# A gated linear recurrence and a top-1 expert layer on one core: transfers with their own planned rates, loads in quarters, heads moved in two long pieces

## The chip, the core and the metric

The kernel runs on one core of a Trainium2 chip. The core has TensorE (PE, with its weight loads shown apart as PEld), VectorE (DVE), ScalarE (ACT), GpSimd (POOL) and SyncE (SP); SP does nothing here but issue DMAs, in the order in which they stand in its queue. The metric is the device time of one execution in microseconds (us), lower being better. All data is float32.

## The reference, cut to what matters

The first half is a recurrence over 768 steps for 4 batches x 8 heads x 48 channels; its output, with heads side by side, is 3072 tokens of 384 values. The second half sends each token to the one expert (of 8) with the highest gate logit.

```python
mag = np.sqrt(a_re * a_re + a_im * a_im)
scale = np.minimum(mag, 0.999) / (mag + 1e-06)          # a = a * scale
for t in range(S):                                      # S = 768
    S_re, S_im = ar*S_re - ai*S_im + k v^T,  ar*S_im + ai*S_re
    y[:, :, t] = einsum('bhd,bhde->bhe', q[:, :, t], S_re)
x = y.transpose(0, 2, 1, 3).reshape(B * S, H * D)       # 3072 x 384
logits = x @ w_gate;  e = argmax(logits);  g = softmax(logits)[e]
out = g * (relu(x @ w1[e]) @ w2[e])                     # w1 384x1024, w2 1024x384
```

## The kernel before, in words

**Attention.** The recurrence is done in chunks of 128 steps: within a chunk by matrices, between chunks by a state. The sequence work is cut into ten units (`UNITS`): u0 (128 steps), u1 (256), six full units u2 to u7 of 384 steps, u8 (256) and u9 (128). For each unit `front(u)` loads a_re and a_im in one DMA into the tile `AB`, and q and k in one DMA into `Z` (`ld`, line 280); there are two buffers of each, shown as AB_124 and Z_126 for even units and AB_125 and Z_127 for odd ones. Then ACT, DVE and POOL turn the gates into magnitudes and angles: Ln and Exp on ACT, the product im*c on POOL, a square with its maximum on DVE (line 291), Ln, an add (295), Exp, a clamp (299), the running sum `D` (scan, line 301), two Exp, the products K on DVE and Q on POOL (the latter the last reader of `AB`), the arc tangent, the running angle `cs` (scan, line 312), sine and cosine. Four DVE products per unit write `zp` (line 326): part 1 (imaginary) from the sine, then part 0 from the cosine, each for k and q. `zp`, `D` and `cs` have one buffer each.

**Moves.** The channels stand on 128 partitions in blocks (`BLOCKS`), the matrix work wants each head on 96 rows. So ten DMAs per unit, five for each part, move `zp` to `hz` inside SBUF (line 333): four of 48 partitions, two of 32, four of 16. `hz` has two buffers (hz_147, hz_148). `chunk(b, c)` then does the matrix work of each of the 24 chunks on PE: transposes of k (line 363), scores (370), state reads (382), values (389), state update (397) and the turn to tokens with the logits (405). DVE masks the scores into `am`, ACT copies the rest. `route` finds each token's expert and place, and POOL scatters the rows to `xs_hbm` (line 467).

**Order.** Nothing of this is ordered by hand. `Plan` collects operations with an engine, a duration, a latency and, for transfers, kilobytes; `order()` makes a list schedule over all engines, in which transfers share one wire at 0.30 KB per ns (`RATE`), and the kernel emits the instructions in the order of the planned starts. `after=` adds a pure ordering: the loads of unit u are planned after the moves of unit u-2.

**Experts.** Between the two halves a check (lines 513 to 536) finds whether a general, slow path must be run (it is not run here); its tiles come from a pool `chkp`, in the memory that the attention's tiles leave, and the expert tiles then use the same memory. For each expert rows `xr` and weights `w1b`, `w2b` are loaded, rows are transposed (587), multiplied by w1 (598), by w2 (612), scaled and scattered to the output. This half is ordered by a second `Plan`.

Of the kernel before, what the change touches and what calls it, by code (L numbers as in the profile page):

```python
# [9 lines left out]
FP32 = mybir.dt.float32  # L10
# [12 lines left out]
G = 3  # L23
# [20 lines left out]
class Plan:  # L44
# [5 lines left out]
    def add(self, eng, dur, fn, r=(), w=(), tag=None, lat=0.0, kb=0.0, prio=0.0, port=False, after=()):  # L50
# [16 lines left out]
        self.ops.append(dict(i=i, eng=eng, dur=dur, fn=fn, deps=sorted(deps), tag=tag, lat=lat, kb=kb, bump=prio, port=port, after=after,  # L67
# [3 lines left out]
    XL, TBL, RATE, SLACK = 0.12, 1.3, 0.30, 0.05  # L71
# [13 lines left out]
    def tails(self, succ):  # L85
        tail = [0.0] * len(self.ops)
        for o in reversed(self.ops):
            t = max([us + tail[s] for s, us, data in succ[o["i"]] if data], default=0.0)
            tail[o["i"]] = t + o["dur"] + o["kb"] / self.RATE / 1e3 + o["bump"]
        return tail  # L90

    def run(self, prio, edges, ins, back, stick):
# [4 lines left out]
        cur, dma, per_kb = None, 0.0, 1 / self.RATE / 1e3  # L97
# [5 lines left out]
        for _ in ops:  # L103
# [27 lines left out]
            if o["kb"] and not back:  # L131
                dma = end = max(dma, end) + o["kb"] * per_kb
            for s, us, data in edges[i]:
                ready[s] = max(ready[s], end + us + (ops[s]["kb"] * per_kb if back else 0.0) if data else issued)
                n[s] -= 1
                if n[s] == 0:
                    cand[ops[s]["eng"]].append(s)
# [19 lines left out]
def gateloop_then_moe(ctx, tc, gates, qk, v, wg, w1, w2, out):  # L157
# [57 lines left out]
    with ExitStack() as att:  # L215
# [8 lines left out]
        zp, = buf("zp", 1, [128, 2, TU // 128, 2, G, 128])  # L224
# [6 lines left out]
        hz = buf("hz", 2, [96, TU // 128, 2, H, 128])  # L231
# [29 lines left out]

        def front(u):
# [16 lines left out]
            def ld(o, src, keys):  # L279
                P.add("SP", 0.65, lambda: nc.sync.dma_start(o[:, :, :, sl], src[b, :, :, :, t0:t1]), (), keys, lat=1.5, kb=2 * n * 0.512, after=moved[u - 2] if u > 1 else ())  # L280
# [43 lines left out]
            for part, key, tr in ((1, Sk, si), (0, ("co",), co)):  # L324
                for x, xk, src in ((1, K, kk), (0, Q, qq)):
                    P.add("DVE", dve2(n), lambda part=part, tr=tr, x=x, src=src: tt(
                        zp[:, part, 0:nch, x].rearrange("p c g t -> p g c t"), src.rearrange("p g (c t) -> p g c t", t=128),
                        tr.rearrange("p g (c t) -> p g c t", t=128), ALU.mult), (xk,) + tuple(key), (("zp", part, x),), port=True)
            for part in (1, 0):
                for p0, p1, g0, g1, h0, d0 in BLOCKS:  # L330
                    m, r0 = g1 - g0, part * D + d0
                    eng, dma = ("ACT", nc.scalar) if u == 0 and part == 0 and h0 else ("SP", nc.sync)
                    i = P.add(eng, 0.65, lambda dma=dma, p0=p0, p1=p1, g0=g0, g1=g1, h0=h0, r0=r0, m=m, part=part: dma.dma_start(
                        hz[slot][r0:r0 + p1 - p0, cl:cl + nch, :, h0:h0 + m].rearrange("p c x h t -> p (c x) h t"),
                        zp[p0:p1, part, 0:nch, :, g0:g1].rearrange("p c x g t -> p (c x) g t")),
                        (("zp", part, 0), ("zp", part, 1)), tuple(("h", slot, cl + x, h, part, d0) for x in range(nch) for h in range(h0, h0 + m)),
                        lat=1.6, kb=2 * (p1 - p0) * m * T * 4 / 1e3)
# [7 lines left out]
        def chunk(b, c):  # L345
# [7 lines left out]
            hq, hk = hz[slot][:, cl, 0], hz[slot][:, cl, 1]  # L353
# [60 lines left out]
        def route(b, r0, r1):  # L414
# [50 lines left out]
            for c in range(n):  # L465
# [6 lines left out]
                P.add("POOL", 1.27, f, (slot, ("xg", (g0 + c) % XR), ("empty", 0), ("empty", 1), ("empty", 2)), (("rows", b, r0 + c),), lat=2.0, kb=197)  # L472
# [14 lines left out]
        with tc.manual_schedule():  # L487
            for u in range(NU):
# [4 lines left out]
                if u == 3:  # L493
                    for h in range(3):
                        P.add("SP", 0.65, lambda h=h: nc.sync.dma_start(
                            xs_hbm.rearrange("(e s) w -> s e w", e=E)[MINC + 64 * h:MINC + 64 * h + 64],
                            bc(empty[0:64, None, :], [64, E, W])), (), (("empty", h),), lat=2, kb=E * 64 * W * 4 / 1e3, after=moved[1])
                for c in range(t0 // 128, t1 // 128):
                    chunk(b, c)
# [12 lines left out]
    with ExitStack() as fs:  # L512
        fp = fs.enter_context(tc.tile_pool(name="chkp", bufs=1, reuse_waits="tile"))
        ok = fp.tile([128, 4], FP32, name="ok")
        f1 = fp.tile([128, NU], FP32, name="f1")
        nc.vector.tensor_scalar(out=f1, in0=chk, scalar1=2.25, scalar2=None, op0=ALU.is_le)
        nc.vector.tensor_reduce(ok[:, 0:1], f1, axis=AX, op=ALU.min)
        lv = lend.rearrange("p b g c -> p (b g) c")
        f2 = fp.tile([128, B * G, C], FP32, name="f2")
        tt(f2, lv[:, :, 1:], lv[:, :, :C], ALU.subtract)  # L520
        nc.vector.tensor_scalar(out=f2, in0=f2, scalar1=-60.0, scalar2=None, op0=ALU.is_ge)
        nc.vector.tensor_reduce(ok[:, 1:2], f2.rearrange("p a c -> p (a c)"), axis=AX, op=ALU.min)
        f3 = fp.tile([128, B * G], FP32, name="f3")
        nc.vector.tensor_scalar(out=f3, in0=lv[:, :, C], scalar1=-100.0, scalar2=None, op0=ALU.is_ge)
        nc.vector.tensor_reduce(ok[:, 2:3], f3, axis=AX, op=ALU.min)
        nc.tensor.matmul(bank[7][:, 0:E], lhsT=ones_b, rhs=cumb, start=True, stop=True)
        f4 = fp.tile([128, E], FP32, name="f4")
        nc.vector.tensor_scalar(out=f4, in0=bank[7][:, 0:E], scalar1=float(CAP), scalar2=None, op0=ALU.is_le)
        f5 = fp.tile([128, E], FP32, name="f5")
# [264 lines left out]
```

## Time and profile before

| | us |
|---|---|
| median of 3 runs | 621.64 (617.7 to 622.54) |
| the profiled execution | 618.8 |
| its span, first to last instruction | 617.0 |
| span of the attention half, to its last matrix work | about 293 |
| pause of TensorE between the halves | 297.7 to 306.8 |
| expert half | 310 to 617 |

| engine | busy in the span | share |
|---|---|---|
| PE | 520.4 | 84% |
| DVE | 261.0 | 42% |
| ACT | 207.6 | 34% |
| POOL | 104.3 | 17% |

Busy shares mix two halves with different limits, so each half is read by itself. "Idle before" a row, and the releaser named with it, say what the engine waited for. The DMA share is the mean busy share of the core's 16 DMA engines; it counts a packet that waits for memory as busy. PEclk is the granted TensorE clock as a share of full speed: 0.50 is 1.2 GHz, 1.00 is 2.4 GHz.

### The profile page before, as it was taken

What the parts mean: (1) busy time and instruction counts of PE and PEld (TensorE: products, weight loads), DVE (VectorE), ACT (ScalarE), POOL (GpSimd) and SP (SyncE); (2) the same over time, 40 slices, a digit from 0 to 9 for tenths busy, and PEclk for the clock granted to TensorE, in tenths of its full rate; (3) what the DMA queues carried; (4) which work ended last, traced back from release to release, by engine and by line L of the source; (5) the groups of instructions that cost most, each with busy time, mean ns of one, the idle gap of its engine ahead of it and who ended that gap; (6) DMA issues with size and microseconds to landing.
All of it is one profiled execution on the core that took longest, in us unless ns stands there. A gap on an engine that the chain in (4) does not pass through costs nothing. (4 is left out here: it accounts for less than half of the span.)

```text
span 617.0 us, 7130 instructions
## 1 busy us (share of the span) xinstructions
PE 520.4 (84%) x2785; PEld 361.0 (59%) x2785; DVE 261.0 (42%) x460; ACT 207.6 (34%) x287; POOL 104.3 (17%) x112
## 2 busy tenths in 40 slices
PE   0269179976979695999199999999999999999996
PEld 0259169865868695988155555555555555555553
DVE  4957955995865954884212021111111111111111
ACT  6665755873847464774011000110001100011000
POOL 5113022303411214233200011100101011100011
PEclk9999655975957668799589999999999999999999
DMA  6584597758797948263795041630425301310000
GB/s 193 159 217 161 107 238 131 216 106 203 181 284 169 174 129 202 55 147 111 268 406 195 13 163 49 242 109 13 167 93 196 109 25 65 115 56 1 13 35 31
DMA packets 47080, 85.57 MB, mean 139 GB/s; under 512 B 3760, under 2 KB 42704, under 8 KB 44992
## 3 DMA queue, kind: packets, MB, share of 16 engines
q1 hardware_dynamic: 43424, 75.33, 44.2%
q0 software_dynamic: 3328, 9.47, 4.3%
q8 instruction: 24, 0.39, 0.3%
q10 hardware_dynamic: 288, 0.25, 0.2%
q14 instruction: 16, 0.13, 0.1%
HBM read 54.32 MB, written 12.62 MB: 109 GB/s over the span
## 5 line engine op out<-in xcount | busy, mean ns | idle before, releaser
L598 PE MATMUL bank<-xrt,w1b 128*128 128x448 f32 x384 | 148.4, 542 | 0.0
L612 PE MATMUL bank<-w2b,ht 128*128 128x384 f32 x384 | 127.5, 488 | 0.0
L598 PEld LDWEIGHTS bank<-xrt,w1b 128*128 128x128 f32 x384 | 73.3, 192 | 68.4 <-issue 64.7
L612 PEld LDWEIGHTS bank<-w2b,ht 128*128 128x128 f32 x384 | 72.5, 190 | 50.5 <-issue 4.1
L370 PE MATMUL bank<-hz 96*128 96x128 f32 x384 | 71.7, 352 | 32.9 <-DMA hz<-zp 31.6
L370 PEld LDWEIGHTS bank<-hz 96*128 96x128 f32 x384 | 64.2, 255 | 39.0 <-issue 24.0
L604 ACT ACTIVATE ht<-bank 128x448 f32<-128x448 f32 x32 | 17.4, 543 | 178.6 <-PE bank L598 178.6
L556 POOL DMA_INDIRECT out_dram<-yo,xr x24 | 23.5, 980 | 283.4 <-DVE yo L567 280.9
L601 DVE TENSOR_SCALAR ht<-bank 128x448 f32<-128x448 f32 x32 | 20.0, 624 | 111.1 <-PE bank L598 104.2
L363 PE MATMUL bank<-ident,hz 96*128 96x96 f32 x160 | 26.3, 314 | 38.3 <-DMA hz<-zp 38.3
L567 DVE TENSOR_SCALAR yo<-bank,xr 128x384 f32<-128x384 f32 x24 | 14.8, 618 | 103.2 <-PE bank L612 103.2
L363 PEld LDWEIGHTS bank<-ident,hz 96*128 96x128 f32 x160 | 21.5, 186 | 41.3 <-issue 31.9
L507 ACT ACT_TABLE_LOAD x35 | 44.9, 1283 | 1.4 <-PEq L782 0.8
L170 DVE TENSOR_TENSOR am<-bank,causal 128x512 f32<-128x512 f32 x48 | 32.2, 685 | 29.3 <-PE bank L370 29.2
L170 DVE TENSOR_TENSOR zp<-Z,cs 128x1152 f32<-128x1152 f32 (+2 forms) x40 | 42.6, 1111 | 0.7 <-ACT cs L254 0.6
L170 POOL TENSOR_TENSOR Z<-Z,AB 128x1152 f32<-128x1152 f32 (+2 forms) x9 | 22.5, 2504 | 102.3 <-ACT AB L254 51.6
L397 PEld LDWEIGHTS bank<-v,kt 128*96 128x96 f32 x320 | 36.8, 202 | 3.4 <-issue 2.8
L397 PE MATMUL bank<-v,kt 128*96 128x48 f32 x320 | 38.4, 284 | 0.4 <-ACT sb L401 0.4
L170 POOL TENSOR_TENSOR AB<-AB,C 128x1152 f32<-128x1152 f32 (+2 forms) x9 | 22.0, 2446 | 98.1 <-ACT C L254 86.6
L589 ACT COPY xrt<-bank 128x384 f32<-128x384 f32 x16 | 7.6, 478 | 86.4 <-PE bank L587 86.4
L405 PE MATMUL bank<-turn,yt 128*128 128x104 f32 x192 | 33.4, 330 | 3.3 <-ACT xg L409 1.8
L389 PE MATMUL bank<-am,v 128*48 128x128 f32 x384 | 33.9, 328 | 0.0
(112 smaller groups left out, 517.1 us busy)
## 6 DMA issues: line engine op xcount, KB each, us to landing
w1b<-in_w_dram SPq DMA_DIRECT2D x8, 1536.0 KB, 7.4
w2b<-in_w_dram SPq DMA_DIRECT2D x8, 1536.0 KB, 8.5
hz<-zp SPq DMA_DIRECT2D x24, 432.0 KB, 6.7
AB<-in_gates_dram SPq DMA_DIRECT2D x6, 1152.0 KB, 6.6
Z<-in_qk_dram SPq DMA_DIRECT2D x6, 1152.0 KB, 10.5
xr<-xs_hbm SPq DMA_DIRECT2D x8, 579.0 KB, 3.8
v<-in_v_dram SPq DMA_DIRECT2D x8, 576.0 KB, 10.2
xs_hbm<-empty SPq DMA_DIRECT2D x3, 772.0 KB, 13.2
```

The costliest lines, as they stand in the source:

```text
L170: (eng or nc.vector).tensor_tensor(out=o, in0=a, in1=b, op=op)
L363: nc.tensor.transpose(KT[hf][:, (h % 4) * 96:(h % 4) * 96 + 96], hk[:, h], ident[0:96, 0:96])
L370: nc.tensor.matmul(SC[hf][:, (h % 4) * 128:(h % 4) * 128 + 128], lhsT=hk[:, h], rhs=hq[:, h], start=True, stop=True)
L389: nc.tensor.matmul(YT[ps, (h // 2) * 128:(h // 2) * 128 + 128], lhsT=V[:, cl, h * D:h * D + D], rhs=am[2 * par + hf][:, h % 4, :], start=( ...
L397: nc.tensor.matmul(ST[0:96, h * D:h * D + D], lhsT=kt[par][:, h * 96:h * 96 + 96], rhs=V[:, cl, h * D:h * D + D], start=(c == 0 and h == 0 ...
L405: nc.tensor.matmul(XT[:, p * 104:p * 104 + 104], lhsT=yt[par][:, p * 128:p * 128 + 128], rhs=turn[:, p, :], start=True, stop=True)
L507: nc.scalar.preload_act_table_set("natural_log_exp_and_others" if P.cur == "LE" else "trig_and_small")
L556: i = nc.gpsimd.indirect_dma_start(out=out[:, :], out_offset=bass.IndirectOffsetOnAxis(ap=index, axis=0), in_=y, in_offset=None, bounds_ch ...
L598: nc.tensor.matmul(HB[hb][:, 0:CAP], lhsT=w1b[ws][:, c:c + 128], rhs=xrt[s][:, d, :], start=(d == 0), stop=(d == DT - 1))
L601: M.add("DVE", 0.6, lambda f_=f_, hb=hb: nc.vector.tensor_scalar_max(ht[s][:, f_, :], HB[hb][:, 0:CAP], 0.0), (("H", hb),), (("ht", s, f_),))
L604: M.add("ACT", 0.6, lambda f_=f_, hb=hb: nc.scalar.activation(ht[s][:, f_, :], HB[hb][:, 0:CAP], func=ACT.Relu), (("H", hb),), (("ht", s, ...
L612: nc.tensor.matmul(OB[ob][:, 0:DM], lhsT=ht[s][:, f_, j * 128:j * 128 + 128], rhs=w2b[ws][:, f_ * DM:f_ * DM + DM], start=(f_ == 0), stop= ...
```

## The change

Five things change. (1) The planner's `kb` and common rate become `wire`, a time of its own for each kind of transfer: loads at 0.32, moves at 0.213 KB per ns, values 1.9 us, weights 4.0 us instead of 5.2. (2) A load of a unit becomes two DMAs, one for each of a_re, a_im, q, k, and the inputs lie in HBM by half sequences, so that a partition's row of a full unit is one run of 4608 bytes and not three of 1536; the `after=` of the loads and of the values is gone. (3) `zp` and `hz` hold a full unit as (part of q or k, head, step), so that a move has two pieces of up to 4608 bytes per partition and not six of up to 1536; partial units keep the old layout. (4) The check's tiles come from `consts`, memory of their own. (5) The general path reads the new input layout.

```diff
-    XL, TBL, RATE, SLACK = 0.12, 1.3, 0.30, 0.05
+    XL, TBL, SLACK = 0.12, 1.3, 0.05
-            if o["kb"] and not back:
-                dma = end = max(dma, end) + o["kb"] * per_kb
+            if o["wire"] and not back:
+                dma = end = max(dma, end) + o["wire"]
...
+        def operand(t, full, z, c):
+            if full:
+                return t.rearrange("p (z h t) -> p z h t", z=2, h=H)[:, z, :, c * 128:c * 128 + 128]
+            return t.rearrange("p (c z h t) -> p c z h t", z=2, h=H, t=128)[:, c, z]
...
             def ld(o, src, keys):
-                P.add("SP", 0.65, lambda: nc.sync.dma_start(o[:, :, :, sl], src[b, :, :, :, t0:t1]), (), keys, lat=1.5, kb=2 * n * 0.512, after=moved[u - 2] if u > 1 else ())
+                for x in range(2):
+                    P.add("SP", 0.65, lambda x=x: nc.sync.dma_start(
+                        o[:, x, :, sl], src[b, t0 // TU, :, x, :, t0 % TU:t0 % TU + T]), (), keys[x:x + 1], lat=1.6, wire=n * 0.000512 / 0.32)
...
+                        if T == TU:
+                            o, i = o.rearrange("p (z x) -> p z x", z=2), i.rearrange("p (z x) -> p z x", z=2)
+                            dma.dma_start(o[:, :, h0 * T:(h0 + m) * T], i[:, :, g0 * T:g1 * T])
...
-                        lat=1.6, kb=2 * (p1 - p0) * m * T * 4 / 1e3)
+                        lat=1.6, wire=2 * (p1 - p0) * m * T * 4e-6 / 0.213)
...
-            P.add("SP", 0.08, lambda: nc.sync.dma_start(
-                vb[i % 3], v[b, 3 * half:3 * half + 3].rearrange("c p f -> p c f")), (), (("v", i % 3),), lat=1.9, kb=590, after=moved.get(2 * b + half - 1, ()))
+            P.add("SP", 0.65, lambda: nc.sync.dma_start(
+                vb[i % 3], v[b, 3 * half:3 * half + 3].rearrange("c p f -> p c f")), (), (("v", i % 3),), lat=1.6, wire=1.9)
...
-        fp = fs.enter_context(tc.tile_pool(name="chkp", bufs=1, reuse_waits="tile"))
-        ok = fp.tile([128, 4], FP32, name="ok")
+    ok = consts.tile([128, 4], FP32, name="ok")
...
-            M.add("SP", 0.65, lambda: nc.sync.dma_start(w1b[ws], w1[e * 128:e * 128 + 128, :]), (), (("w1", ws),), lat=1.9, kb=1573,
+            M.add("SP", 0.65, lambda: nc.sync.dma_start(w1b[ws], w1[e * 128:e * 128 + 128, :]), (), (("w1", ws),), lat=1.9, wire=4.0,
```

**SP's queue in the middle of the attention half.** Before, from the loads of u4 (AB_124, Z_126) to those of u5 (AB_125, Z_127), with the ten moves of u3 (into hz_147) between them; a load is a whole unit:

```order
L280 DMA AB_124<-in_gates_dram 128x6x384
L280 DMA Z_126<-in_qk_dram 128x6x384
L342 DMA v_133<-in_v_dram 128x3x384
L333 DMA hz_147<-zp_132 48x6x384 x2
L333 DMA hz_147<-zp_132 32x6x256
L333 DMA hz_147<-zp_132 16x6x128 x2
L333 DMA hz_147<-zp_132 48x6x384 x2
L333 DMA hz_147<-zp_132 32x6x256
L333 DMA hz_147<-zp_132 16x6x128 x2
L280 DMA AB_125<-in_gates_dram 128x6x384
L280 DMA Z_127<-in_qk_dram 128x6x384
```

Now, around the ten moves of u2 (into hz_148); AB_124 and Z_126 are loads of u4, AB_125 of u5, and each row is a half:

```order
L287 DMA AB_124<-in_gates_dram 128x1152
L350 DMA hz_148<-zp_132 48x2x1152 x2
L350 DMA hz_148<-zp_132 32x2x768
L350 DMA hz_148<-zp_132 16x2x384 x2
L287 DMA AB_125<-in_gates_dram 128x1152
L287 DMA Z_126<-in_qk_dram 128x1152
L350 DMA hz_148<-zp_132 48x2x1152 x2
L350 DMA hz_148<-zp_132 32x2x768
L350 DMA hz_148<-zp_132 16x2x384 x2
L287 DMA Z_126<-in_qk_dram 128x1152
L361 DMA v_133<-in_v_dram 128x3x384
L287 DMA AB_125<-in_gates_dram 128x1152
```

The gates of u4 stand ahead of the moves of u2 and no longer behind them, the first half of u5's gates stands between the two parts of u2's moves, where before it stood behind all of u3's.

**DVE between the products `zp` of u2 and those of u3.** Rows that write cs or D at 128x384 are the scans. Before, the last product of u2 (Z_126) and the twelve rows from it on; the products of u3 come four rows later:

```order
L170 TENSOR_TENSOR zp_132<-Z_126,cs_131 128x3x3x128
L312 SCALAR_TENSOR_TENSOR cs_131<-bank_68,tend,AB_125 128x384 x3
L299 TENSOR_SCALAR AB_125<-AB_125 128x1152
L301 SCALAR_TENSOR_TENSOR D_130<-AB_125,lend,C_129 128x384 x3
L283 COPY tend<-cs_131 128x3x3
L317 TENSOR_SCALAR cs_131<-cs_131 128x1152
L318 SCALAR_TENSOR_TENSOR cs_131<-cs_131 128x1152
L320 TENSOR_SCALAR cs_131<-cs_131 128x1152
L170 TENSOR_TENSOR Z_127<-Z_127,C_129 128x1152
L411 TENSOR_REDUCE lg<-bank_67 128x8
L170 TENSOR_TENSOR am_138<-bank_61,causal 128x512
L170 TENSOR_TENSOR am_139<-bank_62,causal 128x512
```

Now, from the last two products of u2 to those of u3:

```order
L170 TENSOR_TENSOR zp_132<-Z_126,cs_131 128x1152 x2
L303 SCALAR_TENSOR_TENSOR AB_124<-C_128,AB_124 128x1152
L170 TENSOR_TENSOR Z_127<-Z_127,C_129 128x1152
L325 TENSOR_SCALAR cs_131<-cs_131 128x1152
L326 SCALAR_TENSOR_TENSOR cs_131<-cs_131 128x1152
L430 TENSOR_REDUCE lg<-bank_67 128x8 x2
L328 TENSOR_SCALAR cs_131<-cs_131 128x1152
L307 TENSOR_SCALAR AB_124<-AB_124 128x1152
L309 SCALAR_TENSOR_TENSOR D_130<-AB_124,lend,C_128 128x384 x2
L170 TENSOR_TENSOR am_138<-bank_61,causal 128x512
L309 SCALAR_TENSOR_TENSOR D_130<-AB_124,lend,C_128 128x384
L170 TENSOR_TENSOR zp_132<-Z_127,cs_131 128x1152 x4
```

Both scans of u3 (from AB_125) have moved ahead of the last products of u2; in their place stand the add, the clamp and one scan of u4 (AB_124).

**SP's queue at the head of the expert half.** Before, the first row is w1's first load:

```order
L573 DMA w1b_2011<-in_w_dram 128x3072
L576 DMA xr_2017<-xs_hbm 128x3x386
L579 DMA xr_2017<-xs_hbm 64x386
L576 DMA xr_2018<-xs_hbm 128x3x386
L575 DMA w2b_2014<-in_w_dram 128x3072
```

Now the first expert's rows come first:

```order
L593 DMA xr_2039<-xs_hbm 128x3x386
L590 DMA w1b_2033<-in_w_dram 128x3072
L596 DMA xr_2039<-xs_hbm 64x386
L593 DMA xr_2040<-xs_hbm 128x3x386
L592 DMA w2b_2036<-in_w_dram 128x3072
```

The load of w1 has moved behind the rows that the last scatter writes.

## Rows read from the trace of the kernel before

**Rows 1.** Busy time in three stretches: start:end, length, PE, PEld, DVE, ACT, POOL, PEclk, DMA share, GB/s.
```profile
0.00:293.00 293.00, 214.96 (x1788) 194.69 (x1789) 211.51 (x348) 182.19 (x238) 73.72 (x80) 0.80 0.69 168
310.00:617.00 307.00, 301.69 (x980) 163.73 (x978) 44.80 (x82) 23.75 (x46) 27.43 (x28) 0.99 0.28 103
```
**Rows 2.** Who waited for whom, attention half: total us, times, longest.
```profile
POOL AB L170 <- ACT C L254: 86.6, 8, 21.1
...
PE bank L370 <- DMA hz<-zp: 31.6, 9, 14.9
...
SPq L333 <- DVE zp L170: 122.1, 11, 22.5
```
**Rows 3.** SP's queue in time: start, length, what, count.
```profile
94.51 14.33 SPq L333 DMA_DIRECT2D hz<-zp  x10
108.94 0.60 SPq L280 DMA_DIRECT2D AB<-in_gates_dram  x1
...
160.00 14.67 SPq L333 DMA_DIRECT2D hz<-zp  x10
174.77 0.60 SPq L280 DMA_DIRECT2D AB<-in_gates_dram  x1
```
**Rows 4.** Timeline of POOL: u5's product with Q, idle time before, releaser.
```profile
139.49 2.75 POOL L170 TENSOR_TENSOR Z<-Z,AB 128x1152 f32<-128x1152 f32 x1 [15.62 <-issue]
```
**Rows 5.** Timeline of DVE: its first unit work, the last products of u2, u3, u7.
```profile
6.58 0.56 DVE L170 TENSOR_TENSOR AB<-AB,C 128x384 f32<-128x384 f32 x1 [4.67 <-ACT C L254]
...
69.61 1.35 DVE L170 TENSOR_TENSOR zp<-Z,cs 128x1152 f32<-128x1152 f32 x1
...
99.94 2.62 DVE L170 TENSOR_TENSOR zp<-Z,cs 128x1152 f32<-128x1152 f32 x2
...
231.30 1.33 DVE L170 TENSOR_TENSOR zp<-Z,cs 128x1152 f32<-128x1152 f32 x1
```
**Rows 6.** Busy time in stretches cut at those products, columns as in rows 1.
```profile
102.56:232.63 130.07, 108.66 (x920) 98.33 (x920) 99.67 (x140) 80.79 (x105) 28.70 (x18) 0.73 0.77 183
232.63:293.00 60.37, 52.50 (x545) 47.76 (x544) 39.09 (x109) 36.23 (x60) 20.37 (x21) 0.89 0.52 128
```
**Rows 7.** Busy time in the densest stretches of DVE, columns as in rows 1.
```profile
15.00:75.00 60.00, 32.79 (x216) 29.64 (x216) 48.05 (x66) 42.59 (x47) 10.14 (x5) 0.93 0.59 160
...
45.00:75.00 30.00, 19.38 (x146) 17.83 (x146) 25.39 (x29) 22.46 (x25) 5.21 (x2) 0.86 0.50 139
...
105.00:135.00 30.00, 25.97 (x275) 23.32 (x274) 26.96 (x30) 24.75 (x31) 5.75 (x2) 0.90 0.62 167
```
**Rows 8.** Busy time while moves run, then while loads run, columns as in rows 1.
```profile
67.00:84.00 17.00, 2.46 (x10) 2.22 (x11) 16.74 (x18) 9.44 (x9) 3.17 (x1) 0.50 0.97 150
84.00:91.00 7.00, 7.00 (x43) 6.31 (x43) 1.43 (x3) 4.46 (x5) 0.00 (x0) 0.50 1.05 357
```
**Rows 9.** Groups by line: busy us, mean ns of one, idle before.
```profile
L507 ACT ACT_TABLE_LOAD x35 | 44.9, 1283 | 1.4 <-PEq L782 0.8
```
**Rows 10.** Timeline between the halves, with idle time before and its releaser.
```profile
296.52 0.99 POOL L467 DMA_INDIRECT xs_hbm<-xg,slot  x1 [1.01 <-DVE f L521]
...
297.72 0.36 SPq L573 DMA_DIRECT2D w1b<-in_w_dram  x1
300.11 0.38 SPq L576 DMA_DIRECT2D xr<-xs_hbm  x1
...
306.76 3.84 PE L587 MATMUL bank<-ident,xr 128*128 128x128 f32 x15 [9.11 <-DMA xr<-xs_hbm]
...
310.40 15.08 PE L598 MATMUL bank<-xrt,w1b 128*128 128x448 f32 x37
```
**Rows 11.** DMA issues over the span: count, KB each, median us from issue to landing.
```profile
w1b<-in_w_dram SPq DMA_DIRECT2D x8, 1536.0 KB, 7.4
...
AB<-in_gates_dram SPq DMA_DIRECT2D x6, 1152.0 KB, 6.6
...
xr<-xs_hbm SPq DMA_DIRECT2D x8, 579.0 KB, 3.8
```

More of the change, by code (lines that the diff above doesn't have):

```diff
@@ L48, in __init__, with add @@
         self.ops, self.last, self.readers = [], {}, {}
-    def add(self, eng, dur, fn, r=(), w=(), tag=None, lat=0.0, kb=0.0, prio=0.0, port=False, after=()):
+    def add(self, eng, dur, fn, r=(), w=(), tag=None, lat=0.0, wire=0.0, prio=0.0, port=False, after=()):
         i = len(self.ops)
@@ L130, in run @@
             cur = o["tag"] or cur
-            if o["kb"] and not back:
-                dma = end = max(dma, end) + o["kb"] * per_kb
+            if o["wire"] and not back:
+                dma = end = max(dma, end) + o["wire"]
             for s, us, data in edges[i]:
-                ready[s] = max(ready[s], end + us + (ops[s]["kb"] * per_kb if back else 0.0) if data else issued)
+                ready[s] = max(ready[s], end + us + (ops[s]["wire"] if back else 0.0) if data else issued)
                 n[s] -= 1
@@ L351, in chunk @@
             V = vb[i % 3]
-            hq, hk = hz[slot][:, cl, 0], hz[slot][:, cl, 1]
+            hq, hk = (operand(hz[slot], full, z, cl) for z in range(2))
             def hkey(hs):
@@ L471, in f @@
                     tc.add_to_no_dep_group("rows", i.ins)
-                P.add("POOL", 1.27, f, (slot, ("xg", (g0 + c) % XR), ("empty", 0), ("empty", 1), ("empty", 2)), (("rows", b, r0 + c),), lat=2.0, kb=197)
+                P.add("POOL", 1.27, f, (slot, ("xg", (g0 + c) % XR), ("empty", 0), ("empty", 1), ("empty", 2)), (("rows", b, r0 + c),), lat=2.0, wire=0.6)
         def setup():
@@ new lines, in gateloop_then_moe @@
+    nc.vector.tensor_reduce(ok[:, 1:2], f2.rearrange("p a c -> p (a c)"), axis=AX, op=ALU.min)
+    f3 = consts.tile([128, B * G], FP32, name="f3")
+    nc.vector.tensor_scalar(out=f3, in0=lv[:, :, C], scalar1=-100.0, scalar2=None, op0=ALU.is_ge)
+    nc.vector.tensor_reduce(ok[:, 2:3], f3, axis=AX, op=ALU.min)
+    nc.tensor.matmul(bank[7][:, 0:E], lhsT=ones_b, rhs=cumb, start=True, stop=True)
+    f4 = consts.tile([128, E], FP32, name="f4")
+    nc.vector.tensor_scalar(out=f4, in0=bank[7][:, 0:E], scalar1=float(CAP), scalar2=None, op0=ALU.is_le)
@@ new lines, in gateloop_then_moe @@
+    f5 = consts.tile([128, E], FP32, name="f5")
+    nc.vector.tensor_scalar(out=f5, in0=bank[7][:, 0:E], scalar1=float(MINC), scalar2=None, op0=ALU.is_ge)
+    tt(f4, f4, f5, ALU.mult)
+    nc.vector.tensor_reduce(ok[:, 3:4], f4, axis=AX, op=ALU.min)
+    okm = consts.tile([128, 1], FP32, name="okm")
+    nc.vector.tensor_reduce(okm, ok, axis=AX, op=ALU.min)
+    nc.tensor.matmul(bank[7][0:1, 64:65], lhsT=okm, rhs=one, start=True, stop=True)
+    nc.vector.tensor_scalar(out=again, in0=bank[7][0:1, 64:65], scalar1=127.5, scalar2=None, op0=ALU.is_lt)
```

80 lines of the change are left out of this document (36 added, 44 removed).

## The prediction

> **What bounds the kernel now.** The busy time by stretches comes first [rows 1]. The expert half is TensorE's alone: 301.69 us of work in 307, at a granted clock of 0.99. No edit touches that work, so that half keeps its time, and all that can move lies in the attention half and in the pause between the halves. In the attention half no engine is full: PE has 214.96 of 293 us, DVE 211.51, ACT 182.19, the DMA engines 0.69. So a chain bounds it, and the waits must name it. They go round in a circle [rows 2]: POOL waits 86.6 us for ACT's Exp, which starts a unit; PE waits 31.6 us for moved heads at the scores alone; SP waits 122.1 us, with moves in hand, for DVE's products.
>
> SP's queue shows how the circle closes [rows 3]. The ten moves of u3 are issued from 94.51 to 108.9, and only then, at 108.94, the gates of u5. u5's own moves start at 160.00, and behind them, at 174.77, go the gates of u7. From load to load that is 65.8 us for two units, 32.9 us for each: 51.1 us from load to moves and 14.7 us of moves. The reader should see that the second load need not have waited for this. POOL's product with Q, the last reader of u5's gates, ends at 139.49 + 2.75 = 142.2 [rows 4]. The buffer then lies free for 32.5 us until u7's load is issued. The pace, taken from the ends of the products of u3 (102.56) and u7 (232.63) [rows 5], is 130.07 us for four units, 32.5 each. In it DVE works 99.67 us, 24.9 per unit, and ACT 20.2 [rows 6].
>
> **Loads that no longer stand behind moves.** The order shows u4's gates ahead of u2's moves, and half of u5's gates between the two parts of those moves. A load now goes out about when its buffer is free, up to 32 us sooner, and its first half carries a_re, which is all that ACT needs to begin. A whole load lands in 6.6 us [rows 11], half of it in less. So the circle is cut, and the next limit is an engine's queue. Candidates per unit: DVE 24.9, ACT 20.2, and PE, which has 108.66 us there, 27.2 per unit, but is elastic: at clock 0.50 (1.2 GHz) 43 matmuls keep it busy 7.00 us [rows 8], at 0.90 275 take 25.97 [rows 7], 163 against 94 ns each. Shorter pauses bring the clock back, so I take DVE as the limit that stays.
>
> The order confirms what DVE gets from it. Before, between the products of u2 and those of u3 stand both scans of u3 and all that waits for them; that stretch takes from 70.96 to 102.56 [rows 5]. Now both scans stand ahead of u2's last products, and work of u4 fills the gap. DVE does not get less work: 172.42 of its 211.51 us stand before the end of u7's products (all but the 39.09 behind it [rows 6]), and both orders have 14 masking products behind that point. It waits less. DVE starts at 6.58 [rows 5], so before it did this work in 226 us, 76% busy. How busy can it get, in a queue that takes its instructions in order and has the masks of PE's scores among them? The densest minute of before, 15 to 75 us, has 48.05 of 60, 80%; the densest half minutes 85% and 90% [rows 7]. I take 85%, the middle of the three: 6.6 + 172.42/0.85 = 209.4 instead of 232.6, a gain of **23.2 us**. Bounds: 78% gives 227.6 (5 us), 90% gives 198.2 (34 us).
>
> What follows u7's products, 60.37 us, is set by PE, which has 52.50 us of work there [rows 6]. I leave it as it is (bounds: 0 to 5 us better, for moves that land sooner).
>
> **Table loads and issues.** The new order has 41 table loads on ACT in this half against 35: 6 x 1.283 = 7.7 us [rows 9]. ACT would then have 190 us of work in some 270, and its work of a unit with them 21 us against 24.9 on DVE, so I cost them at nothing; if ACT were the limit they would cost the 7.7. Twenty more DMAs at 0.60 [rows 3] are 12 us on SP, which waits 122.1 us anyway; what they can cost is order, below.
>
> **Longer pieces.** While u2's moves run, the DMA engines are 0.97 busy and carry 150 GB/s; right behind, loads with the same pieces of 1536 bytes run at 357 [rows 8]. So the short piece alone does not make moves slow. The Trainium skill ("DMA: Bandwidth & Descriptors", section "Why small descriptors are slow (HBM only)") says that SBUF-to-SBUF transfers do not suffer from small descriptors; the two rates agree with that, and no run here shows moves with other pieces. By that rule the moves keep their 17 us a unit and this edit gives nothing; by the planner's new rate the 2.55 MB of that stretch would take 12 us, and the sum would be up to 5 us lower. In the sum itself I use neither: moves of a middle unit lie beside 25 us of other work, and those of the last units are the bound above.
>
> **Between the halves.** Before, the first load of w1 waits for the check and goes out at 297.72; the rows go out at 300.11, when the last scatter (296.52) has landed, and share the wire with it, so that TensorE starts at 306.76 and with w1 at 310.40 [rows 10]. With tiles of its own the check no longer holds w1, but the new order puts w1 behind the rows, which wait for the scatter anyway: the freed wait is not used. Rows alone land in 3.8 us [rows 11], 303.9; w1, 0.4 us later, needs 7.4, 307.9; the last 64 rows come behind it, about 308.5, and their transpose and copy take 0.8. TensorE starts w1 near 309.3, 1.1 us sooner. Ten small DVE instructions of the check, some of which stood before the last scatter, give at most 0.7 more. I take **1.5 us** (bounds: 3 better, 4 worse if w1 lands late).
>
> **Sum**, against the profiled execution's 618.8: 618.8 - 23.2 - 1.5 = 594.1, rounded to **594 us**. The median of the runs is 2.8 us above that execution; the spread of 617.7 to 622.54 is in the range.
>
> **Rivals.**
> *Only the start gains.* PE's clock may set the pace. After a wait of 14.9 us for heads, the longest of its line [rows 2], it works at 0.50 [rows 8], and the masks on DVE then wait for PE. If each unit still begins with a gap and half-speed work, the pace of 32.5 stays, and only the stretch before the end of u3's products gains: 172.42 - 99.67 = 72.75 us of DVE's work, which at the 80% of the densest minute [rows 7] ends at 6.6 + 90.9 = 97.5 and not at 102.6. Time: 618.8 - 5.1 - 1.5 = 612. For it: clock 0.73 over the steady stretch [rows 6]. Against it: from 105 to 135, at clock 0.90, DVE kept 90% [rows 7].
> *All engines close up.* DVE at 90% and a shorter end: 618.8 - 34.4 - 5 - 1.5 = 578.
> *SP's queue holds the moves.* Slower than before. The queue is in order, and u5's gates now stand ahead of the second part of u2's moves. That load waits for POOL's product of u3, which waits for ACT; POOL has waited for ACT for up to 21.1 us [rows 2]. While it waits, five moves wait behind it, then PE, at half speed after. Six units have such a place; the gain of 24.7 is gone at 4.1 us per unit, and at 6 us the time is 618.8 - 24.7 + 36 = 630. Against it: in the new orders eight ACT instructions stand between u2's cosine and the Exp that POOL's product of u3 waits for, and DVE has u2's last two products, for which the held moves wait, behind some ten instructions of its own; the two should end within a few us of each other.
> *Nothing changes.* If the circle through loads was not the limit, because DVE's waits for ACT within a unit are, time is 618.8 - 1.5 = 617.
>
> **Numbers.** Chances: forecast (585 to 603) 0.50, only the start 0.15, all close up 0.15, queue holds 0.10, nothing changes 0.10. The range takes the first three: 575 to 613. Changes of under 1% (6 us) can't be told from none here. Faster by over 1%, below 615.4: 0.50 + 0.15 + 0.15 = 0.80. Within 1%: 0.10. Slower: 0.10.
>
> **What would show it.** Right: SP's queue issues the gates of a unit within a few us of POOL's product with Q of the unit two before; the products of u7 end near 209; DVE is about 85% busy until then; four units take near 117 us. TensorE starts w1 about 9 us after the rows' issue. Wrong: the products still come every 32.5 us; or moves are issued long after their products are done, with a load ahead of them that waits for POOL; or the second half is no longer 302 us.

## The result, and the profile after

The changed kernel takes **592.82 us** (median of 4 runs, 588.52 to 601.41) against 620.26 (4 runs, 617.7 to 622.54) for the kernel before beside it: a ratio of 0.954, 95% interval 0.943 to 0.964. A second set of runs (6 of the changed kernel, 11 of the kernel before), with which the experiments are compared, gave 592.58 against 620.88: 0.951, 0.944 to 0.958. Faster, as forecast, and 1.2 us from the forecast of 594. Ratios and their intervals leave out the runs that lie furthest above the fastest of their kernel; medians and ranges have all runs.

Two executions of it were profiled: one of 601.4 us (span 599.6) and one of 588.0 (span 586.3). Views are of the second, unless the first is named. Its stretches, to TensorE's last matrix work of the attention half and from its first matmul with w1, answer to [rows 1]; columns as there:

```profile
0.00:261.20 261.20, 197.73 (x1788) 179.72 (x1789) 211.66 (x355) 189.82 (x243) 76.13 (x80) 0.86 0.73 188
277.80:586.30 308.50, 303.23 (x980) 163.74 (x980) 44.65 (x81) 23.79 (x46) 27.37 (x28) 0.99 0.29 105
```

TensorE's work in the expert half is as it was (301.69 us in [rows 1]), though from the first matmul with w1 to the end it is 308.5 us and not 306.6 (617.0 - 310.40). In the attention half the 1788 matmuls of [rows 1] now take 197.73 us and not 214.96, and the time that TensorE stands idle falls from 78.0 (293 - 214.96) to 63.5. So the 31.8 us between the two rows are 17.2 of quicker matmuls, which goes with the granted clock (0.80 to 0.86), and 14.6 of idle time. DVE's work is the same. In the first profile the half ends at 274.64:

```profile
0.00:274.64 274.64, 212.09 (x1788) 192.58 (x1789) 211.02 (x355) 189.90 (x243) 75.48 (x80) 0.81 0.70 179
```

There the matmuls take 212.09 us at a clock of 0.81, and the 18.4 us gained are 2.9 of quicker matmuls and 15.5 of idle time. Both executions have the gain in idle time; the one in matmuls changes from execution to execution.

The same cut at the ends of DVE's products, u2 to u3, u3 to u7, and from there on, answers to [rows 6]; below them u3 to u7 in the first profile:

```profile
73.25:90.94 17.69, 11.39 (x61) 10.94 (x60) 14.79 (x18) 13.02 (x14) 0.00 (x0) 0.54 0.90 219
90.94:202.01 111.07, 102.42 (x972) 92.30 (x971) 95.15 (x145) 83.36 (x108) 33.08 (x20) 0.84 0.85 209
202.01:261.20 59.19, 51.57 (x550) 47.15 (x550) 38.94 (x109) 33.72 (x56) 18.32 (x19) 0.91 0.51 131
```

```profile
90.45:215.46 125.01, 115.04 (x971) 103.72 (x971) 94.64 (x144) 83.36 (x108) 32.28 (x20) 0.75 0.77 185
```

A unit takes 27.8 us in the one execution (111.07 / 4) and 31.3 in the other, where it took 32.5. The same 971 or 972 matmuls keep TensorE busy for 102 us at a clock of 0.84 and for 115 at 0.75, and the stretch is longer by 13.9. That is all of the 13.4 us between the two executions. TensorE is 92% busy in the stretch in both, DVE 86% and 76%; before it was 84% and 77% [rows 6].

The waits (total us, times, longest; answering to [rows 2]):

```profile
POOL AB L170 <- ACT C L254: 70.7, 6, 19.6
PE bank L389 <- DMA hz<-zp: 29.6, 2, 27.6
SPq L350 <- DVE zp L170: 24.7, 7, 12.0
SPq L353 <- DVE zp L170: 19.0, 3, 10.8
```

SP waits 43.7 us (24.7 + 19.0) with moves in hand for those products, where it waited 122.1; all its waits with moves in hand, whatever releases them, sum to 62 us where they were 127. TensorE waits long for heads only once, at the very start. SP's queue and POOL around the loads of u7, answering to [rows 3] and [rows 4]; the two rows of AB are the halves of u7's gates, the five moves are u4's and the ten are u5's:

```profile
122.74 0.37 SPq L287 DMA_DIRECT2D AB<-in_gates_dram  x1
125.10 5.77 SPq L350 DMA_DIRECT2D hz<-zp  x5
130.91 0.59 SPq L287 DMA_DIRECT2D Z<-in_qk_dram  x1
131.60 1.49 SPq L287 DMA_DIRECT2D AB<-in_gates_dram  x1
...
142.41 11.88 SPq L350 DMA_DIRECT2D hz<-zp  x10
```

```profile
124.41 3.15 POOL L170 TENSOR_TENSOR Z<-Z,AB 128x1152 f32<-128x1152 f32 x1 [2.01 <-ACT AB L254]
```

POOL's product with Q of u5, the last reader of u5's a_re, ends at 127.56 (124.41 + 3.15). The first half of u7's gates goes out before that, so it is a_im; a_re goes out at 131.60, 4.0 us behind the product, where the whole load went out 32.5 behind it. Over u4 to u9 it is 0.0 to 11.3 us, before 17.5 to 32.5.

### The profile page after: what moved, and what is told of

Its sections match the earlier page's. It is cut to its first block, busy times and chain, and to the rows that moved or that the text cites. A ratio compares the mean times of both kernels' runs of the same rounds, so it can differ in the third digit from the quotient of the medians.

```text
span 599.6 us, 7162 instructions
## 1 busy us (share of the span) xinstructions
PE 518.8 (87%) x2785; PEld 358.6 (60%) x2785; DVE 259.8 (43%) x460; ACT 215.3 (36%) x293; POOL 106.1 (18%) x112
## 5 line engine op out<-in xcount | busy, mean ns | idle before, releaser
L615 PE MATMUL bank<-xrt,w1b 128*128 128x448 f32 x384 | 150.1, 547 | 0.5 <-issue 0.5
L389 PE MATMUL bank<-hz 96*128 96x128 f32 x384 | 69.9, 345 | 37.9 <-DMA hz<-zp 34.3
L389 PEld LDWEIGHTS bank<-hz 96*128 96x128 f32 x384 | 62.5, 249 | 42.5 <-DMA hz<-zp 31.9
L424 PE MATMUL bank<-turn,yt 128*128 128x104 f32 x192 | 34.7, 338 | 14.2 <-ACT xg L428 6.6
L424 PEld LDWEIGHTS bank<-turn,yt 128*128 128x128 f32 x192 | 30.7, 243 | 18.0 <-ACT xg L428 7.1
L486 POOL DMA_INDIRECT xs_hbm<-xg,slot x24 | 26.3, 1095 | 45.4 <-DVE cum L170 15.4
L170 POOL TENSOR_TENSOR Z<-Z,AB 128x1152 f32<-128x1152 f32 (+2 forms) x9 | 22.1, 2451 | 51.1 <-ACT AB L254 50.5
```

Source lines behind the costliest of these rows:

```text
L170: (eng or nc.vector).tensor_tensor(out=o, in0=a, in1=b, op=op)
L389: nc.tensor.matmul(SC[hf][:, (h % 4) * 128:(h % 4) * 128 + 128], lhsT=hk[:, h], rhs=hq[:, h], start=True, stop=True)
L424: nc.tensor.matmul(XT[:, p * 104:p * 104 + 104], lhsT=yt[par][:, p * 128:p * 128 + 128], rhs=turn[:, p, :], start=True, stop=True)
L486: i = nc.gpsimd.indirect_dma_start(out=xs_hbm[:, :], out_offset=bass.IndirectOffsetOnAxis(ap=R[slot][:, c:c + 1], axis=0), in_=xg[:, (g0 + ...
L615: nc.tensor.matmul(HB[hb][:, 0:CAP], lhsT=w1b[ws][:, c:c + 128], rhs=xrt[s][:, d, :], start=(d == 0), stop=(d == DT - 1))
```

## The experiments

Ratios are against runs of the kernel before on the same chip, with 95% intervals; times of different sets of runs are compared through these ratios, since the kernel before took 620.9, 622.2 and 626.7 us in the three sets.

**The changed kernel again.**

> The changed kernel itself, unchanged, for a second profile of it. Every theory expects 589 to 596 us and a ratio of 0.95 to 0.96. What is asked of the profile: the products of u7 end near 209 us as the prediction said, or later (215.5 in the first profile); TensorE's granted clock in the steady stretch (0.75 in the first profile); and the time from the rows' issue to TensorE's first matmul with w1 (9.5 us in the first profile).

Measured: 592.58 us (584.85 to 614.42), products of u7 at 202.0, clock 0.84 in the steady stretch, 9.4 us from the rows' issue to w1. One and the same kernel spreads over 30 us, where the kernel before beside it spreads over 8.7.

**The order of loads alone, and the change without it.** First the kernel before with

```diff
-lat=1.5, kb=2 * n * 0.512, after=moved[u - 2] if u > 1 else ())
+lat=1.5, kb=2 * n * 0.512)
```

and the like for v; then the changed kernel with `after=` put back in both places.

> The kernel before with one edit: its loads of gates, Q and K, and v are no longer planned behind the moves of an earlier unit. Rates, whole loads, short pieces and the check's tiles stay. Theory 'the order of loads' (the prediction's): this edit alone gives most of the gain, 595 to 603 us, ratio 0.96 to 0.975, and the products of u3 end near 90 us instead of 102.6. Rival 'rates and pieces': the order is not the limit, because moves with short pieces still take 17 us of a unit; 613 to 619 us, ratio 0.99 to 1.0. Rival 'halves': without a first half that lands early the load still comes too late for ACT; 606 to 612.

> The changed kernel with the loads of gates, Q, K and v planned behind the moves of an earlier unit again, as before. Theory 'the order of loads': the circle of load, front chain, moves and next load is back, the pace is 32 to 33 us per unit, and the time is 611 to 619 us (2.1 to 1.0 below before for the pause between the halves and the quicker moves). Rival 'rates and pieces': 590 to 600 us, since moves with pieces of 4.6 KB shorten the circle by 5 us per unit (17 to 12), which over five units is the whole gain.

Measured: 612.42 us, 0.978 (0.971 to 0.984), for the order alone; 603.18, 0.965 (0.957 to 0.972), without it. For the order alone the rival 'halves' (606 to 612) comes nearest; for the change without it neither theory has it. The order alone gives a little less than half of the gain, and the change keeps some 70% of its gain without it. With the loads behind moves again TensorE is idle for 73.1 us of the half, but its matmuls stay at 197.80:

```profile
0.00:270.88 270.88, 197.80 (x1788) 178.55 (x1789) 209.16 (x355) 171.44 (x229) 73.25 (x80) 0.84 0.69 181
```

In that run the circle is whole: u5's gates, u5's ten moves, u7's gates.

```profile
106.49 2.43 SPq L287 DMA_DIRECT2D AB<-in_gates_dram  x2
...
146.71 16.35 SPq L350 DMA_DIRECT2D hz<-zp  x10
163.16 1.01 SPq L287 DMA_DIRECT2D AB<-in_gates_dram  x2
```

But from u5's load to its moves it takes 40.2 us and not 51.1 [rows 3], and the four units from u3 to u7 take 111.6 us, as in the second profile of the changed kernel (111.07). What this run loses against that profile it loses ahead of them (5.3 us) and in the tail (3.8). So a good part of the gain is a quicker way from a unit's load to its moves, with the load as late as ever. Which part of the change makes it quicker was not separated.

**Pieces.** The layout of whole units as in the change, put into the kernel before in its own order; and the short pieces put into the changed kernel (`if T == TU:` made `if False:`, `chunk(b, c, False)`).

> The kernel before with one edit, in the same order: the operands of whole units lie as in the changed kernel, so that their heads move in pieces of 4608 bytes and not 1536. Theory 'pieces give nothing' (the prediction's, and the Trainium skill's page 'DMA: Bandwidth & Descriptors', section 'Why small descriptors are slow (HBM only)'): 618 to 622 us, ratio 0.995 to 1.0. Rival 'pieces shorten the circle': moves of a unit take some 12 us instead of 17, and as the kernel before waits for them in each unit, 2 to 3 us of a unit come off in five units and the start: 604 to 610.

> The changed kernel with the same order of instructions, but the operands laid out by chunk in every unit, so that moves run in pieces of 1536 bytes as before. Theory 'pieces give nothing' (the prediction took none of it, and the Trainium skill's page 'DMA: Bandwidth & Descriptors', section 'Why small descriptors are slow (HBM only)', says that SBUF to SBUF does not suffer): within 2 us of the changed kernel, 589 to 596. Rival 'pieces matter': moves of a unit take 17 us again and not some 12, the heads come up to 5 us later in each of five units, TensorE's gaps grow and its clock falls: 600 to 615.

Measured: 1.000 (0.995 to 1.004) for the long pieces alone: nothing. The moves of u2 in the kernel with long pieces, in the stretch of [rows 8]:

```profile
67.00:84.00 17.00, 3.14 (x13) 2.90 (x14) 16.90 (x18) 9.68 (x10) 3.17 (x1) 0.50 0.89 164
```

164 GB/s at 0.89 of the DMA engines, against 150 at 0.97, and SP's ten issues of these moves take 11.71 us as against 11.92. TensorE gets the heads of u2 a little sooner: its first two groups on them start 11.3 and 15.1 us behind the first issue (78.67 and 82.48, issue at 67.42), before 12.2 and 16.0 (79.35 and 83.17, issue at 67.18). That is 0.9 us and not 5. The rule of the Trainium skill ("DMA: Bandwidth & Descriptors", section "Why small descriptors are slow (HBM only)"), that SBUF-to-SBUF transfers do not suffer from small descriptors, agrees with this run for pieces of 1536 and 4608 bytes. In the changed kernel the short pieces gave 602.51 us (585.33 to 607.85; median against median 0.970, no interval): the median lies in the range of the rival 'pieces matter', perhaps 10 us worse, unresolved in that spread. One sign speaks for the rival. From 60 to 230 us TensorE waits 15.7 us for heads in the profile with short pieces, and 7.5 in the second profile of the changed kernel (6.9 in the first); short pieces first:

```profile
PE bank L389 <- DMA hz<-zp: 9.2, 4, 3.0
PE bank L382 <- DMA hz<-zp: 6.5, 3, 3.3
```

```profile
PE bank L382 <- DMA hz<-zp: 5.4, 4, 2.8
PE bank L389 <- DMA hz<-zp: 2.1, 1, 2.1
```

**Halves and rates.** The changed kernel with whole loads (one DMA for both halves of a tile, `wire` doubled), and with the one old rate in the plan (`/ 0.30` for loads and moves, and the old numbers for values and scatters).

> The changed kernel with a unit's gates in one load and Q and K in one load again, not in halves; the planner sets its order anew. Theory 'halves only let SP's queue interleave, the order of loads does the work': 590 to 597 us. Rival 'the first half that lands early matters': ACT starts each unit 1.5 to 3 us later, 598 to 606.

> The changed kernel planned by the one rate of before for every transfer (0.30 instead of 0.32 for loads and 0.213 for moves, so a unit's moves count 8.5 us in the plan and not 12). Theory 'the order of loads, not the numbers': 590 to 597 us. Rival 'the plan with its own rate for moves keeps TensorE from waiting': heads come later than planned, TensorE pauses, its clock stands longer at half: 598 to 610.

Measured: 618.66 us, 0.984 (0.977 to 0.991) with whole loads: two thirds of the gain are gone, more than any other part costs and more than either theory expected. 604.75 us, 0.966 (0.960 to 0.972) with the old rate, in the range of its rival. In both the planner writes another order on every engine, so these two show what the part is worth together with the order that goes with it. With whole loads the matmuls are slow again (210.97 us) and idle time is 78.4:

```profile
0.00:289.32 289.32, 210.97 (x1788) 189.85 (x1789) 220.61 (x355) 169.27 (x227) 80.22 (x83) 0.81 0.66 171
```

Whole loads are not late. Here u6's gates go out as soon as POOL's product of u4 ends (120.48 + 2.64 = 123.12):

```profile
120.48 2.64 POOL L170 TENSOR_TENSOR Z<-Z,AB 128x1152 f32<-128x1152 f32 x1 [18.00 <-issue]
```

```profile
123.15 0.33 SPq L286 DMA_DIRECT2D AB<-in_gates_dram  x1
```

Over u4 to u9 they go out 0.0 to 8.3 us behind that product, and 0.0 to 8.6 in the run with the order alone, no later than a_re in the changed kernel. So the wait behind the moves is gone in these two runs as well, and they have only a third and not quite half of the gain.

**Which engine sets the pace now.** In the changed kernel's own order, DVE without the two sine products from u3 on (moves then carry old values), and TensorE without the product of state and queries from the second batch element on:

```diff
+                    if u > 2 and part == 1:
+                        f = lambda: None
                     P.add("DVE", dve2(n), f, (xk,) + tuple(key), ...
```

```diff
+                if i > 1:
+                    f = lambda: None
                 P.add("PE", 1.02, f, (("sb", 1 - par),) + ...
```

> The changed kernel with the same order, without two of the four products that DVE makes of a unit (those with the sine), from u3 on; the moves then carry old values. It takes 2 x 1.35 us of DVE's work out of each whole unit, 13.5 us up to the end of u7's products and 16 us in all. Theory 'DVE's queue is the limit now' (the prediction's): 10 to 16 us below the changed kernel, 577 to 583. Rival 'TensorE with its clock is the limit now': 0 to 5 us below, 588 to 592.

> The changed kernel with the same order, without the product of the state with the queries (line 401) from the second batch element on; the outputs leave that part out. It takes 15 groups of eight matmuls from TensorE, 1.0 us each at the full clock and 2 us at half, 17 to 20 us in the profiles of the changed kernel. Theory 'TensorE with its clock is the limit now': 10 to 20 us below the changed kernel, 573 to 583. Theory 'DVE's queue is the limit now': 0 to 5 us below, and these in the last units, where DVE is idle anyway.

Measured: 594.95 us (581.85 to 617.42; 0.9425, 0.935 to 0.950) with less DVE work, 594.59 (583.79 to 605.68; 0.944, 0.937 to 0.951) with less TensorE work. Both theories fall as they stood: by the ratios, 16 us less on one engine, or 17 to 20 on the other, is some 5 us below the changed kernel's 0.951, which the intervals do not tell from nothing. What TensorE no longer has to do it loses at the clock, 0.78 over the half against 0.86 and 0.81 in the two profiles of the changed kernel:

```profile
0.00:265.82 265.82, 202.23 (x1548) 184.50 (x1549) 210.13 (x355) 189.34 (x243) 72.96 (x80) 0.78 0.71 185
```

240 matmuls fewer, and TensorE is busy for 202.23 us, between the 197.73 and 212.09 of the two profiles of the changed kernel.

The single runs say more than their medians. Each run's time against its own mean granted clock:

| kernel | runs | mean us | mean clock | us per 0.01 of clock | correlation |
|---|---|---|---|---|---|
| before (two sets) | 22 | 620.9 | 0.890 | 0.0 | 0.01 |
| changed | 10 | 594.3 | 0.911 | -5.5 | -0.96 |
| before, loads free | 6 | 612.7 | 0.900 | -5.4 | -0.97 |
| changed, loads behind moves | 6 | 603.6 | 0.908 | -2.4 | -0.40 |
| before, long pieces | 12 | 627.9 | 0.878 | -0.9 | -0.55 |
| changed, short pieces | 6 | 600.5 | 0.907 | -5.0 | -0.97 |
| changed, whole loads | 6 | 621.7 | 0.885 | -4.6 | -0.98 |
| changed, old rates | 6 | 605.0 | 0.917 | -3.8 | -0.53 |
| changed, DVE lighter | 6 | 598.1 | 0.908 | -6.0 | -0.99 |
| changed, TensorE lighter | 6 | 594.1 | 0.889 | -5.5 | -0.85 |

The kernel before took 620.9 us at a clock of 0.866 and 621.3 at 0.930. The changed kernel took 614.4 at 0.881 and 584.9 at 0.933. As long as loads stand behind moves the time follows the clock little; once they are free, it follows it in most kernels. On the changed kernel's line a clock of 0.889 would give 606.4 us (594.3 + 5.5 x 2.2); with TensorE lighter it is 594.1, 12.3 less. A clock of 0.908 would give 596.0; with DVE lighter it is 598.1, no gain for 16 us. These are lines through a few runs, of two sets whose kernel before differs by 1.3 us. And a run that waits more might have a low clock for that reason; a row of the first profile speaks against it being only this (columns as in [rows 1]):

```profile
142.00:170.00 28.00, 28.00 (x163) 24.63 (x162) 12.80 (x23) 12.86 (x19) 5.37 (x3) 0.50 0.66 158
```

For 28 us TensorE works without a gap at half the clock, and no other engine has work for half of the time. In the second profile such a stretch lasts 12 us (158 to 170). So TensorE with its clock, more than DVE, is what the changed kernel runs against. That much is argued from rows and lines: no run changed the clock without giving TensorE other work.

**Keeping the clock.** Constant matmuls (128x128, read by nobody) ahead of TensorE's first work with each half sequence but the first, 24 at a place, on PE's queue:

```diff
+                        for _ in range(WARM):
+                            nc.tensor.matmul(bank[7][:, 384:512], lhsT=ident, rhs=ident, start=True, stop=True, ...
```

> The changed kernel with 24 matmuls of 128x128 on a constant ahead of TensorE's first work with the heads of each half sequence but the first; nothing reads their result. They fill the pause in which TensorE otherwise waits for moves (3 to 7 us in the second profile of the changed kernel), behind which its granted clock stood at 0.50 for 5 to 30 us. They cost 5.1 us each at the full clock where there is no pause. Theory 'the clock after the pause sets the time': granted clock in the attention half above 0.95 behind them, time 575 to 586, and less spread between runs. Rival 'DVE is the limit': the clock rises and the time stays within 3 us. Rival 'no pause to fill': 5 us for each of up to seven places, 600 to 625.

> The kernel with 24 constant matmuls ahead of each half sequence, and, between the halves, the first loads of w1 and w2 issued ahead of the rows, the last 64 rows right behind the other rows, and 20 constant matmuls ahead of the first transposes of the rows. Between the halves the prediction's account expects TensorE to start with w1 5.5 to 7 us after the rows' issue, instead of 9.4 in the changed kernel (w1 and the last 64 rows no longer come behind each other); if the wire is not what it waits for, still about 9. In all 2 to 6 us below the kernel with the constant matmuls alone.

> The kernel with constant matmuls ahead of each half sequence but the first and with the first weights ahead of the rows, with 12 constant matmuls at each place instead of 24 (20 between the halves become 12). Theory 'TensorE's busy time at the granted clock sets the time': each place costs 2.6 us and not 5.1, 18 us less over seven places; if the clock holds as with 24, 585 to 591 us with a spread of under 4 us; if 12 are too few to hold it, 588 to 600 with a spread of 10 as in the changed kernel.

Measured: 602.68 us (601.05 to 603.99), 0.971 (0.967 to 0.975). The clock does what was expected and the time does not; it is in the range of the rival 'no pause to fill'. From 90 to 206 us, first with the constant matmuls, then in the changed kernel:

```profile
90.00:206.00 116.00, 112.04 (x1200) 104.07 (x1200) 99.81 (x150) 85.00 (x112) 32.21 (x20) 0.99 0.85 206
```

```profile
90.00:206.00 116.00, 107.34 (x1022) 96.99 (x1022) 99.98 (x152) 85.97 (x112) 36.15 (x23) 0.85 0.86 210
```

At 0.99 instead of 0.85 the engine does the same useful work in the same time (1008 of the 1200 matmuls, the other 192 are constant ones): the constant matmuls fill what the clock gives back. Behind u7's products the tail takes 70.5 us and not 59.2; constant matmuls of two places stand there, 13.0 us. But the spread of six runs falls from 30 us to 2.9: where the clock is held, the spread is gone. With 12 at a place (and the first weights ahead of the rows) it is 602.03, 0.961 (0.955 to 0.967), the spread back at 16. None of these beats the changed kernel.

With the weights ahead (24 at a place) 601.11 us, 0.967, 1.6 us below the constant matmuls alone. Between the halves that edit does a part of what was expected: TensorE's transposes and first matmul with w1, beside the rows' issue at 283.00 and, with 12 at a place, 280.32:

```profile
286.98 0.88 PE L614 MATMUL bank<-ident,xr 128*128 128x128 f32 x6
...
290.75 0.76 PE L614 MATMUL bank<-ident,xr 128*128 128x128 f32 x3 [1.78 <-DMA xr<-xs_hbm]
291.30 0.95 PE L625 MATMUL bank<-xrt,w1b 128*128 128x448 f32 x1
```

```profile
287.49 0.16 DVE L645 COPY hg<-xr 64x2 int32<-64x2 int32 x1 [6.88 <-DMA xr<-xs_hbm]
289.01 0.36 DVE L616 COPY xrt<-bank 128x192 f32<-128x192 f32 x1 [0.56 <-PE bank L614]
```

8.3 us, and 7.0 with 12 at a place (w1 from 287.33), instead of 9.4. The last 64 rows are there at 287.49, and their transposes are copied at 289.01. The wait that is left, 1.78 us, is ahead of three transposes of 128 rows more, which are of the second expert and stand ahead of w1's matmuls in TensorE's order; whether w1 itself was there sooner is not shown.

## Why the prediction was right, point by point

**The expert half keeps its time: right.** 303.23 us of work at 0.99, against 301.69 [rows 1]; to the end of the execution it is 1.9 us longer, which the prediction did not have.

**The circle is cut: right; that the gain is this cut: in part.** a_re of u7 follows POOL's product by 4.0 us and not 32.5, and SP's waits with moves in hand for the products fall from 122.1 to 43.7 us [rows 2]. But the step put the gain down to the order of loads. The order alone gives 0.978, and with whole loads 0.984, though in both the load follows that product as closely. With the loads as late as before, the rest of the change gives 0.965, by a way from load to moves that is 11 us shorter; for this the prediction has no term. Nor does the first half carry a_re: in the planner's order a_im goes ahead of it in seven of the ten units, u5's among them, and ACT begins with the second half. Why halves are worth as much as they are was not separated from the order that the planner writes for them.

**The size, 23.2 us: right in number, by a wrong next limit.** The products of u7 end at 202.0 and 215.5 in the two profiles, 30.6 and 17.2 us sooner than before; forecast 209.4 lies between them, as do 117 us for four units (111.1 and 125.0) and DVE 85% busy (171.85 of 195.11 us from 6.90 on, 88%, in the second profile, 171.24 of 208.96, 82%, in the first). That the forecast lies between two paces which the clock of an execution decides is in part luck. DVE alone is not what holds it there: 16 us less of DVE's work gave no gain that can be told. The step that failed is the one that set TensorE aside as "elastic". It had the clock right (0.50 behind a pause, 163 against 94 ns for a matmul) and then took shorter pauses to bring the clock back by themselves. Pauses did get shorter, from 5.4 us a unit [rows 6] to 2.2 and 2.5, and they still cost the clock. In the changed kernel (4 us each, columns as in [rows 1]):

```profile
154.00:158.00 4.00, 1.96 (x15) 1.55 (x12) 3.25 (x3) 3.14 (x4) 3.37 (x3) 0.83 0.98 233
158.00:162.00 4.00, 4.00 (x25) 3.72 (x24) 3.01 (x4) 2.69 (x3) 3.08 (x4) 0.50 0.99 358
162.00:166.00 4.00, 4.00 (x25) 3.69 (x21) 2.13 (x7) 3.31 (x4) 0.48 (x1) 0.50 1.05 394
166.00:170.00 4.00, 4.00 (x29) 3.54 (x29) 4.00 (x4) 2.20 (x4) 0.00 (x0) 0.50 0.19 70
170.00:174.00 4.00, 4.00 (x41) 4.00 (x40) 0.58 (x3) 2.69 (x4) 0.00 (x0) 0.96 0.66 146
```

The pause is a wait for moved heads:

```profile
154.71 0.47 PE L382 MATMUL bank<-ident,hz 96*128 96x96 f32 x3 [0.42 <-DMA hz<-zp]
156.80 0.39 PE L382 MATMUL bank<-ident,hz 96*128 96x96 f32 x1 [1.62 <-DMA hz<-zp]
```

Two us of pause, then 12 us of full work at half the clock, in which DVE is busy for 9.1. The Trainium skill ("TensorE: Matmul & The Clock Gate", section "HAM oscillation — how this bites in real kernels") says that a wait for a transfer between two bursts throws the clock back, so that the next burst begins cold; the trace agrees, with 25 matmuls in the 4 us behind the pause and 41 in those where the clock comes back. So the rival "only the start gains" had the right engine with wrong prices: it kept the pace at 32.5, and the pace is 27.8 or 31.3, as the clock of a run falls out; and it gave the start 5.1 us, which gained 11.6 and 12.1 (u3's products end at 90.94 and 90.45, before at 102.56).

**The tail behind u7's products, unchanged: right.** 59.19 us against 60.37 [rows 6].

**Table loads and issues at nothing: not contradicted.** ACT has 189.82 us of work in 261, with the 41 loads that were forecast; no run took them alone.

**Pieces at nothing: right where it could be told**, 1.000 in the order of before; open in the new order, where one profile has TensorE wait 8 us more with short pieces.

**The planner's own rates:** the prediction used neither the new rate's 12 us for a unit's moves nor any other price. Undone, they cost 0.966 against 0.951, some 9 us: as numbers of the plan they matter, through the order that it writes.

**Between the halves, 1.5 us: right within its bounds.** SP's queue, TensorE, and the landing of the last 64 rows, which DVE's copy shows, answering to [rows 10]:

```profile
268.39 0.38 SPq L593 DMA_DIRECT2D xr<-xs_hbm  x1
268.83 0.58 SPq L590 DMA_DIRECT2D w1b<-in_w_dram  x1
269.45 0.51 SPq L596 DMA_DIRECT2D xr<-xs_hbm  x1
```

```profile
272.19 2.38 PE L604 MATMUL bank<-ident,xr 128*128 128x128 f32 x9 [6.58 <-DMA xr<-xs_hbm]
276.74 0.56 PE L604 MATMUL bank<-ident,xr 64*128 64x64 f32 x3 [2.17 <-DMA xr<-xs_hbm]
277.80 18.58 PE L615 MATMUL bank<-xrt,w1b 128*128 128x448 f32 x42 [0.50 <-issue]
```

```profile
276.63 0.16 DVE L635 COPY hg<-xr 64x2 int32<-64x2 int32 x1 [2.30 <-DMA xr<-xs_hbm]
```

From the rows' issue to w1 it is 9.4 us (forecast 9.2, before 10.3), so 0.9 us are gained there, and the last 64 rows are there 8.2 us behind that issue (forecast 8.4). The freed wait of w1 is not used, as forecast.

**The rival on the other side**, SP's queue holding the moves behind a load, did not come. u5's moves go out as soon as DVE's two sine products are done (139.77 + 2.62 = 142.39):

```profile
139.77 2.62 DVE L170 TENSOR_TENSOR zp<-Z,cs 128x1152 f32<-128x1152 f32 x2
```

```profile
142.41 11.88 SPq L350 DMA_DIRECT2D hz<-zp  x10
```

Over u2 to u7 the moves go out 0 to some 2 us behind their products. The rival's premise was not met either: the half of u5's gates that stands ahead of the second part of u2's moves is a_im, which does not wait for POOL's product of u3 (it goes out at 69.21, that product ends at 69.49).

## What to carry to other kernels

When a chain through transfers is cut, look at which engine the next limit falls on with the clock that it will really get: an engine that is idle a few us per unit at the chain's old pace has less room than its busy share says, when its clock falls behind each pause. Undo each part of a change by itself, the one that the account calls the cause above all: here most of the gain stayed with the loads put back behind the moves, and only a third to half came of going early. And compare single runs against their granted clock before medians: a time that follows the clock points at TensorE, and a kernel whose runs spread after a change may have come to lean on it.

## What the runs showed of the hardware

- The time of one and the same program follows the granted clock over 30 us (584.9 us at a mean of 0.933, 614.4 at 0.881), and not at all in the kernel before, which waits for transfers (620.9 at 0.866, 621.3 at 0.930).
- Behind pauses of 2.0 and 3.9 us for moved heads, TensorE worked without a gap at a granted clock of 0.50 for 12 us in one execution (158 to 170) and for 28 in the other (142 to 170).
- Less TensorE work went with a lower clock: with 240 of 1788 matmuls fewer the mean over six runs was 0.889 (0.911 over ten runs of the changed kernel), and TensorE was busy for 202.23 us of the half, against 197.73 and 212.09.
- Matmuls that nobody reads hold the clock at 0.99 over 116 us and bring the spread of six runs from 30 to 2.9 us, at some 10 us in the median.
- In the order of before, moves between partitions in pieces three times as long kept the DMA engines 0.89 busy and not 0.97, and their heads reached TensorE 0.9 us sooner.
